# PSUM as one tile of eight banks, MLP units of one bank, and score pieces issued two by two

## The chip, the core and the metric

The kernel runs on one core of a Trainium2 chip. The metric is the device time of one execution in microseconds (us). The core has a matrix engine (TensorE, in the profile PE, and PEld for its weight loads), two engines that read its results out of the accumulation memory PSUM (ScalarE or ACT, VectorE or DVE), a third for work between SBUF tiles (GpSimd or POOL), and SyncE (SP), which here only issues DMAs. PSUM has 128 partitions of eight banks; one bank holds 512 fp32 values for each partition. Engines run their own instruction lists in order and wait for each other through semaphores.

## What is computed

An attention with a few extra keys ("beacons") ahead of the sequence, followed by a two-layer MLP with a squared relu. In short:

```python
# B, H, S, Nb, D = 8, 8, 576, 16, 64;  d_model 512, d_ff 2048
k_all, v_all = concat(beacon_k, k), concat(beacon_v, v)          # 592 keys
a = softmax(q @ k_all.T / sqrt(D), causal on the sequence's keys, beacons always seen)
x = (a @ v_all) as [B*S, H*D]                                    # 4608 tokens x 512
out = (relu(x @ w_in) ** 2) @ w_out                              # 4608 x 512
```

## The kernel before

**Tiling.** Each of the 8 batches is worked in 4 head pairs, so there are 32 pairs. For a pair, PE computes scores transposed (keys on partitions, queries along the row): `qk`, at L506, in matmuls that use 64 of the 128 rows, one head in the upper and one in the lower half. Call this the row form. The scores of a pair come in four *pieces* (batch 0: one and three). A piece holds one or two ranges of queries, so two or four matmuls, and fills a pair of PSUM banks, one bank for each head. ACT takes the exponential of a piece (`exp`, L520), DVE sets masked entries to zero (`mask`, L530 and L534), PE multiplies by v (`av`, L550, 30 matmuls of 65 columns), DVE divides by the sum (`norm`, L565 and L566) into `xn`.

The result of a batch is transposed into the ring `xT`: on PE for batches 0 and 1 (L614), by five DMA transposes on SP for the others (L597). Queries and keys are transposed on PE for batches 0 to 2 (`tp`, L401 and L405, a third form that uses 64 columns), and from batch 3 on they are loaded (L326, L327), cast by POOL (L282) into `qk_area`, and transposed by two DMAs on SP, qT and kT (L359). `qk_area` is first used by PE's transposes; its second use waits for the last of those (a memset on POOL, L306).

The MLP works in 9 chunks of 512 tokens. In the first layer (`s1`, L678) a *unit* is two of the 16 column tiles of w_in, 8 matmuls of 512 columns into a pair of banks; ACT or DVE takes the relu (L694, L696) of 1024 values, and DVE squares it (L703). The second layer (`s2`, L718) adds 16 matmuls for each of 4 groups of 128 tokens; two groups share a pair of banks, ACT copies them out (L280), and SP stores 256 tokens (L750). The last 256 tokens are copied and stored in two halves (L752).

**What sets the order.** A planner (`Order`, L44) plays the program through with a price for each operation and a delay for its result to be seen. At each moment an engine takes the available operation of the lowest number (`prio`); a gate ties the attention's progress to that of the MLP. The order so found is written out, engine by engine, and the chip keeps it. Operations that write PSUM take a buffer from the pool `ps`, four tiles of two banks each, in the order in which they came free; limits say how many each kind may hold:

```python
pools={"ps": range(4), "stg": range(NSTG), "pt": range(NPT)},
limits={"strip": 2, "av": 2, "mlp": 2, "tp": 1},
```

`strip` are the scores, `tp` the transposes. A score piece takes one tile and its exp gives it back (L513 to L524); an MLP unit takes one and its relu gives it back.

Of the kernel before, what the change touches and what calls it, by code (L numbers as in the profile page):

```python
# [9 lines left out]
FP32 = mybir.dt.float32  # L10
# [6 lines left out]
class Op:  # L17
# [4 lines left out]
                 "sync", "insts")  # L22

    def __init__(self, name, engs, dur, emit, prio=0.0, deps=(), take=None, give=None,
                 gate=None, dma=0.0, pe_time=0.0, behind=(), sync=()):
# [12 lines left out]
        self.dma = dma  # L38
        self.pe_time = pe_time
        self.behind = list(behind)  # L40
        self.followers = []


class Order:  # L44
# [3 lines left out]
    LAT = {"PE": 0.2, "ACT": 0.2, "DVE": 0.15, "POOL": 0.25, "SP": 0.1, "-": 0.0}  # L48

    def __init__(self, pools, limits):  # L50
        self.pools = {k: list(v) for k, v in pools.items()}
        self.limits = dict(limits)
        self.inuse = {k: 0 for k in limits}
# [9 lines left out]
    def run(self):  # L63
# [23 lines left out]
        now = 0.0  # L87
        while events:
            now = events[0][0]
            while events and events[0][0] <= now + 1e-9:  # L90
# [6 lines left out]
                elif kind == "give":  # L97
                    pool, cls, idx = op.give.held
                    self.pools[pool].append(idx)
                    if cls in self.inuse:  # L100
                        self.inuse[cls] -= 1
            again = True
            while again:
                again = False
                for e in engines:
# [3 lines left out]
                    fallback = None  # L109
                    for op in avail[e]:  # L110
                        if any(free[x] <= now + 1e-9 for x in op.engs[:op.engs.index(e)]):
                            continue
                        if op.take:
                            pool, cls = op.take
                            if not self.pools[pool]:
                                continue
                            if cls in self.limits and self.inuse[cls] >= self.limits[cls]:
                                continue
# [20 lines left out]
                    if op.take:  # L139
                        pool, cls = op.take  # L140
                        op.held = (pool, cls, self.pools[pool].pop(0))
                        if cls in self.inuse:
                            self.inuse[cls] += 1
                    dur = op.dur[e] if isinstance(op.dur, dict) else op.dur
                    end = now + dur
# [31 lines left out]
def kernel(  # L177
# [64 lines left out]
    ps = [psum.tile([128, 2, 512], FP32, name=f"ps{i}") for i in range(4)]  # L242

    def wait_for(later, first):
# [4 lines left out]
        pools={"ps": range(4), "stg": range(NSTG), "pt": range(NPT)},  # L249
        limits={"strip": 2, "av": 2, "mlp": 2, "tp": 1},  # L250
# [60 lines left out]
    def add_load(b, x, c, prio, behind=[], sync=[]):  # L311
# [10 lines left out]
        def emit_load(e):  # L322
            st = stg[ld.held[2]]
            insts = []
            if lo:
# [6 lines left out]
                 prio=prio, take=("stg", "stg"), dma=1.1 * rows / 128, behind=load_chain[-1:] + behind, sync=sync)  # L332
        load_chain.append(ld)

        def emit_cast(e):
            st = stg[ld.held[2]]
# [40 lines left out]
    def add_strided(b, prio):  # L377
# [17 lines left out]
        for pr in range(HP):  # L395
# [3 lines left out]
            def emit_tp(e, pr=pr, h=h, box=box):  # L399
                pp = ps[box["t"].held[2]].bitcast(BF16)  # L400
                nc.tensor.transpose(pp[:, 1, 0:Nb], bks[b % 2][:, h, :], ident[0:Nb, 0:Nb])  # L401
                for half, at, t in ((1, Nb, ks), (0, 0, qs)):
                    for u in range(NS):
# [5 lines left out]
            tp = add(f"tp{b}.{pr}", "PE", 0.8 if b else 1.3, emit_tp, prio=100.0 * (HP * b + pr) - 190,  # L409
                     deps=[bk, loads[pr, "k"], loads[pr, "q"], ident_op] + busy, take=("ps", "tp"))  # L410
            box["t"] = tp

            def emit_k(e, pr=pr, box=box):
                pp = ps[box["t"].held[2]].bitcast(BF16)
# [4 lines left out]
            def emit_q(e, pr=pr, box=box):  # L419
                pp = ps[box["t"].held[2]].bitcast(BF16)  # L420
# [3 lines left out]
            ek = add(f"ek{b}.{pr}", "DVE", 0.9, emit_k, prio=-200.0, deps=[tp])  # L424
            eq = add(f"eq{b}.{pr}", ("DVE", "ACT"), 0.75, emit_q, prio=-199.0, deps=[tp])
# [50 lines left out]
    def add_pair(b, pr):  # L476
# [12 lines left out]
        take_pt = add(f"pt{p}", "-", 0.0, None, prio=100.0 * p, deps=qk_deps, take=("pt", "pt"), gate=gate)  # L489
# [4 lines left out]
    def add_phase(b, pr, p, n, ph, take_pt, qk_deps, gate):  # L494
        base = 100.0 * p + 1000.0 * n
        exps = []
        for i, (mms, off, width) in enumerate(ph.pieces):
            cols = sum(max(96, t1 - t0) for _, t0, t1, _ in mms)
            box = {}

            def emit_qk(e, mms=mms, box=box):
                st = ps[box["qk"].held[2]]
                for c, t0, t1, at in mms:
                    for hj in range(2):
                        hp = slice(64 * hj, 64 * hj + 64)
                        nc.tensor.matmul(  # L506
                            st[:, hj, at:at + t1 - t0],
                            kT[b % 2][hp, pr, 128 * c:128 * c + 128],
                            qT[b % 2][hp, pr, t0:t1],
                            start=True, stop=True,  # L510
                        )
# [6 lines left out]
            def emit_exp(e, off=off, width=width, box=box):  # L518
                st = ps[box["qk"].held[2]]
                nc.scalar.activation(pt[take_pt.held[2]][:, :, off:off + width], st[:, :, 0:width],  # L520
                                     AF.Exp, bias=0.0, scale=scale)

            exps.append(add(f"exp{p}.{n}.{i}", "ACT", 0.18 + 2 * width / 1200.0, emit_exp, prio=base + i,
                            deps=[qk], give=qk))  # L524

        def emit_mask(e):
            P = pt[take_pt.held[2]]
# [9 lines left out]
        mask = add(f"mask{p}.{n}", "DVE", 0.15 + 0.14 * ph.diag[3] + (0.25 if ph.last else 0.0), emit_mask,  # L537
# [3 lines left out]
        def emit_av(e):  # L541
            P = pt[take_pt.held[2]]
            a = ps[av.held[2]]
            for hj in range(2):
                h = 2 * pr + hj
                for t in tl:
# [10 lines left out]
        av = add(f"av{p}.{n}", "PE", 0.07 + 0.064 * sum(t + 1 for t in tl), emit_av, prio=base - 150,  # L557
                 deps=[mask] + [cast[b, "v", c] for c in range(tl[-1] + 1)] + av_ops[p], take=("ps", "av"),
# [3 lines left out]
        def emit_norm(e):  # L562
            a = ps[av.held[2]][:, :, 0:nt * (D + 1)].rearrange("p h (t d) -> p h t d", d=D + 1)
# [12 lines left out]
        norm_ops[p, n] = add(f"norm{p}.{n}", "DVE", 0.4 + 0.133 * nt, emit_norm, prio=base - 150, deps=deps, give=av)  # L576
# [27 lines left out]
    def add_xt_pe(b):  # L604
        for k, ph in enumerate(phases(b)):
            for pr in range(HP):
# [3 lines left out]
                def emit_tp(e, pr=pr, box=box, ph=ph):  # L610
                    pp = ps[box["t"].held[2]].bitcast(BF16)
                    for t in ph.tiles:
                        n = t_rows(t)
                        nc.tensor.transpose(pp[:, 0, t_start(t):t_start(t) + n],  # L614
# [3 lines left out]
                         deps=[norm_ops[HP * b + pr, k]], take=("ps", "tp"))  # L618
                box["t"] = tp

                def emit_ev(e, pr=pr, box=box, lo=lo, hi=hi):
                    pp = ps[box["t"].held[2]].bitcast(BF16)
                    at = (b * S) % RING
                    copy_on(e, xT[:, pr, at + lo:at + hi], pp[:, 0, lo:hi])

                o = add(f"xte{b}.{k}.{pr}", ("ACT", "DVE"),
                        {"ACT": 0.2 + (hi - lo) / 1200.0, "DVE": 0.12 + (hi - lo) / 960.0}, emit_ev, prio=-110.0,
# [25 lines left out]
    def add_chunk(j):  # L653
# [11 lines left out]
        for f in range(NFT // 2):  # L665
            sqs = []
            for n, (lo_, hi_) in enumerate(parts):
                spans = [(lo_, wrap), (wrap, hi_)] if lo_ < wrap < hi_ else [(lo_, hi_)]
                N = hi_ - lo_
                box = {}  # L670

                def emit_s1(e, f=f, spans=spans, box=box):
                    h = ps[box["s1"].held[2]]
                    for u in range(2):
                        ft = 2 * f + u
                        for lo, hi in spans:
                            for mc in range(NMC):
                                nc.tensor.matmul(h[:, u, lo - spans[0][0]:hi - spans[0][0]],  # L678
# [155 lines left out]
```

## Time and profile before

| | us |
|---|---|
| median of 3 runs (lowest to highest) | 355.35 (355.27 to 355.38) |
| span of the profiled execution | 353.2 |
| PE busy | 334.7 (95%) |
| ACT busy | 193.4 (55%) |
| DVE busy | 148.9 (42%) |
| POOL busy | 85.5 (24%) |

The profiled execution's own time is its span and what lies around it, 2.15 us if it ran like the median. Times in the views count from the span's start. In a timeline a row is start, length, engine, line, operation, tiles, shape and count, and in brackets the idle time before it with what ended it. A matmul's 64*128 are the rows and columns of the array that it uses, and the last shape is what streams through. Ends of matmuls are modelled and overlap the next start, so starts are compared. A few matmul records are missing.

### The profile page before, as it was taken

The page shows a single profiled execution, that of the slowest core. Times are in us where ns is not written, and L with a number is a line of the kernel's source. Part 1 is how long each engine was busy: PE and PEld are TensorE (multiplying, and loading weights), DVE is VectorE, ACT ScalarE, POOL GpSimd, SP SyncE. Part 2 cuts the span into 40 slices and gives each one's busy share as a digit, 9 for nine tenths or more (in the row PEclk, how much of TensorE's full clock was granted, in tenths as well). Part 3 has the DMA queues.
Part 4 walks back from the last instruction along what each step waited for, and adds up shares of the span by engine and source line. Part 5 has one row for each costly group of instructions (what it writes and reads, how often), then busy time and mean ns, then how long its engine had stood idle before and what let it go on. Part 6 is the DMA issues. An engine that isn't in the chain of part 4 may idle for free.

```text
span 353.2 us, 7173 instructions
## 1 busy us (share of the span) xinstructions
PE 334.7 (95%) x2943; PEld 178.6 (51%) x2980; DVE 148.9 (42%) x287; ACT 193.4 (55%) x233; POOL 85.5 (24%) x132
## 2 busy tenths in 40 slices
PE   3789999999999989999999999999999999999994
PEld 2459665554545444444446874445454444444441
DVE  5576674349714455146622753247132302301300
ACT  2686786287555764665745663676634405505602
POOL 7273721209215504133501651000000000000000
PEclk9999999999999999999999999999999999999999
DMA  7999999965969999699989999440013103003003
GB/s 101 183 160 204 223 206 211 201 169 118 206 116 236 223 221 191 138 224 222 251 137 202 248 213 209 115 118 11 0 61 69 59 0 121 0 0 121 0 0 119
DMA packets 137008, 49.49 MB, mean 140 GB/s; under 512 B 123344, under 2 KB 132048, under 8 KB 136976
## 3 DMA queue, kind: packets, MB, share of 16 engines
q1 hardware_dynamic: 127472, 40.09, 53.4%
q0 software_dynamic: 9504, 8.95, 15.7%
q8 instruction: 23, 0.38, 0.5%
q14 instruction: 9, 0.07, 0.1%
HBM read 37.22 MB, written 9.44 MB: 132 GB/s over the span
## 4 chain that ended last, share of the span: by engine, by line
PE 74%; DMA 12%; SPq 5%; ACT 4%; DVE 2%; issue 2%; POOL 1%; ACTq 0%; DVEq 0%; POOLq 0%
PE ps L678 32%; PE ps L718 27%; PE ps L550 7%; PE ps L506 6%; DMA stg<-in_k_dram 4%; DMA stg<-in_v_dram 4%; SPq L597 3%; ACT pt L520 2%; DMA kT<-qk_area 2%; DMA stg<-in_q_dram 1%; SPq L327 1%; DVE kT L282 1%; DMA qk_area<-in_q_dram 1%; PE ps L405 1%; ACT qT L280 1%
## 5 line engine op out<-in xcount | busy, mean ns | idle before, releaser
L678 PE MATMUL ps<-xT,w_in 128*128 128x512 bf16 (+3 forms) x689 | 131.9, 340 | 1.6 <-ACT qT L280 0.6
L718 PE MATMUL ps<-w_out,g 128*128 128x512 bf16 x554 | 129.5, 380 | 1.4 <-issue 0.5
L520 ACT ACTIVATE pt<-ps 128x832 bf16<-128x832 f32 (+4 forms) x128 | 105.3, 865 | 40.7 <-PE ps L506 40.2
L678 PEld LDWEIGHTS <-w_in 128*128 128x128 bf16 x704 | 66.0, 98 | 57.6 <-issue 6.0
L694 ACT ACTIVATE g<-ps 128x1024 bf16<-128x1024 f32 (+2 forms) x65 | 61.8, 951 | 54.0 <-PE ps L678 53.8
L718 PEld LDWEIGHTS <-g 128*128 128x128 bf16 x576 | 53.0, 98 | 65.7 <-issue 5.8
L703 DVE TENSOR_TENSOR g<-g 128x1024 bf16<-128x1024 bf16 (+2 forms) x80 | 53.0, 664 | 77.5 <-ACT g L694 77.0
L530 DVE TENSOR_TENSOR pt<-pt,tri 128x1024 bf16<-128x1024 bf16 (+1 forms) x36 | 24.8, 692 | 50.1 <-ACT pt L520 48.6
L282 POOL CAST qk_area<-stg 128x512 bf16<-128x512 f32 (+2 forms) x50 | 34.6, 704 | 35.0 <-DMA stg<-in_k_dram 18.7
L282 POOL CAST vb<-stg 128x512 bf16<-128x512 f32 (+1 forms) x38 | 26.0, 695 | 69.6 <-DMA stg<-in_v_dram 59.1
L506 PE MATMUL ps<-qT,kT 64*128 64x80 bf16 (+6 forms) x400 | 39.1, 291 | 1.7 <-DMA kT<-qk_area 1.0
L280 ACT COPY osb<-ps 128x1024 f32<-128x1024 f32 (+1 forms) x19 | 18.3, 969 | 40.6 <-PE ps L718 40.3
L550 PEld LDWEIGHTS <-pt 128*128 128x128 bf16 (+1 forms) x960 | 34.5, 99 | 8.8 <-issue 2.5
L550 PE MATMUL ps<-vb,pt 128*128 128x65 bf16 (+1 forms) x960 | 36.5, 196 | 1.9 <-DVE pt L530 0.9
L566 DVE TENSOR_TENSOR xn<-ps,rcp 128x640 bf16<-128x640 f32 (+2 forms) x36 | 27.0, 750 | 1.7 <-DMA xT<-xn 0.4
L506 PEld LDWEIGHTS <-kT 64*128 64x128 bf16 x400 | 13.7, 97 | 24.2 <-issue 18.8
L565 DVE RECIPROCAL rcp<-ps 128x10 f32<-128x10 f32 (+2 forms) x36 | 7.6, 211 | 38.1 <-PE ps L550 36.2
L696 DVE TENSOR_SCALAR g<-ps 128x1024 bf16<-128x1024 f32 (+2 forms) x15 | 15.8, 1053 | 7.8 <-PE ps L678 7.0
L280 ACT COPY qT<-ps 128x576 bf16<-128x576 bf16 x12 | 7.7, 640 | 16.1 <-DVE kT L282 13.0
L282 DVE COPY kT<-ps 128x16 bf16<-128x16 bf16 (+1 forms) x24 | 9.9, 456 | 9.7 <-PE ps L405 7.5
L405 PE MATMUL ps<-ident,qk_area 96*64 96x96 bf16 x288 | 11.1, 233 | 2.9 <-DMA qk_area<-in_k_dram 1.8
L534 DVE TENSOR_TENSOR pt<-pt,tri 80x160 bf16<-80x160 bf16 x32 | 10.8, 339 | 0.0
(31 smaller groups left out, 57.1 us busy)
## 6 DMA issues: line engine op xcount, KB each, us to landing
out_dram<-osb SPq DMA_DIRECT2D x17, 512.0 KB, 3.5
stg<-in_v_dram SPq DMA_DIRECT2D x21, 256.0 KB, 5.1
stg<-in_q_dram SPq DMA_DIRECT2D x20, 256.0 KB, 4.8
stg<-in_k_dram SPq DMA_DIRECT2D x15, 256.0 KB, 5.1
w_in<-in_moe_w_in_dram POOLq DMA_DIRECT2D x4, 512.0 KB, 8.2
w_out<-in_moe_w_out_dram POOLq DMA_DIRECT2D x4, 512.0 KB, 10.6
stg<-in_v_dram SPq DMA_DIRECT2D x7, 224.0 KB, 4.7
qk_area<-in_k_dram POOLq DMA_DIRECT2D x4, 288.0 KB, 12.4
```

The source lines that it names most:

```text
L280: nc.scalar.copy(dst, src)
L282: eng[e].tensor_copy(dst, src)
L506: nc.tensor.matmul(st[:, hj, at:at + t1 - t0], kT[b % 2][hp, pr, 128 * c:128 * c + 128], qT[b % 2][hp, pr, t0:t1], start=True, stop=True,)
L520: nc.scalar.activation(pt[take_pt.held[2]][:, :, off:off + width], st[:, :, 0:width], AF.Exp, bias=0.0, scale=scale)
L530: nc.vector.tensor_tensor(out=d, in0=d, in1=tri[:, m0:m0 + m, :][:, None].to_broadcast([128, 2, m, 128]), op=ALU.min)
L550: nc.tensor.matmul(a[:, hj, (t - tl[0]) * (D + 1):(t - tl[0] + 1) * (D + 1)], P[0:rr, hj, o:o + 128], vb[b % 2][0:rr, c, h, :], start=(c = ...
L566: nc.vector.tensor_tensor(out=xn[b % 2].rearrange("p t (h d) -> p h t d", d=D)[:, 2 * pr:2 * pr + 2, tl[0]:tl[0] + nt], in0=a[:, :, :, 0:D ...
L678: nc.tensor.matmul(h[:, u, lo - spans[0][0]:hi - spans[0][0]], w_in_sb[:, mc, ft * 128:(ft + 1) * 128], xT[:, mc, lo % RING:lo % RING + hi ...
L694: nc.scalar.activation(dst, h, AF.Relu, bias=0.0, scale=1.0)
L696: nc.vector.tensor_scalar(out=dst, in0=h, scalar1=0.0, scalar2=None, op0=ALU.max)
L703: nc.vector.tensor_tensor(out=d, in0=d, in1=d, op=ALU.mult)
L718: nc.tensor.matmul(o[:, ts, :], G[:, fc, (2 * u + ts) * 128:(2 * u + ts + 1) * 128], w_out_sb[:, fc, :], start=(fc == 0), stop=(fc == NFT ...
```

## The change

PSUM becomes one tile of eight banks. A new pool, `Banks`, gives out single banks or aligned pairs: a pair is the lowest free one; a single bank is one whose partner is taken, the lowest of those, or else the lowest free. Limits are counted in banks (scores, attention results and MLP 4 each, transposes 2), and while an operation that wants two pairs lacks banks, operations behind it in rank may bring the MLP to 2 banks only (`floors`).

An MLP unit is now one column tile: 4 matmuls into one bank, with its own relu of 512 values; the square is still taken over two tiles. Each of the 4 token groups of the second layer has its own bank and its own copy out. For chunk 0 the four groups now advance together, quarter by quarter of w_out; before, the first two ended ahead of the last two.

For batches 1 to 7 the scores of a pair are issued as two operations of two pieces each; each takes two pairs of banks, and each of its exps gives back one.

In the planner the delays and prices change, and PE's price gets 0.096 us more wherever the form of its matmuls changes (`mode`).

```diff
+class Banks:
+    def __init__(self):
+        self.free = set(range(8))
+
+    def find(self, wants):
+        left = set(self.free)
+        got = []
+        for n in wants:
+            if n == 2:
+                pick = next((b for b in range(0, 8, 2) if b in left and b + 1 in left), None)
+            else:
+                pick = min(left, key=lambda b: (b ^ 1 in left, b), default=None)
+            if pick is None:
+                return None
+            got.append(pick)
+            left -= {pick, pick + 1} if n == 2 else {pick}
+        return got
...
-    LAT = {"PE": 0.2, "ACT": 0.2, "DVE": 0.15, "POOL": 0.25, "SP": 0.1, "-": 0.0}
+    LAT = {"PE": 0.2, "ACT": 0.15, "DVE": 0.12, "POOL": 0.15, "SP": 0.1, "-": 0.0}
+    DRAIN = 0.096
...
+                            if cls in self.limits:
+                                most = self.limits[cls]
+                                if short is not None and op.prio > short:
+                                    most = min(most, self.floors.get(cls, most))
+                                if self.inuse[cls] + sum(wants) > most:
+                                    continue
...
+                    if e == "PE":
+                        dur += self.DRAIN * (mode not in (None, op.mode))
+                        mode = op.mode
...
-    ps = [psum.tile([128, 2, 512], FP32, name=f"ps{i}") for i in range(4)]
+    ps = psum.tile([128, 8, 512], FP32, name="ps")
...
-        pools={"ps": range(4), "stg": range(NSTG), "pt": range(NPT)},
-        limits={"strip": 2, "av": 2, "mlp": 2, "tp": 1},
+        pools={"ps": Banks(), "stg": Slots(NSTG), "pt": Slots(NPT)},
+        limits={"strip": 4, "av": 4, "mlp": 4, "tp": 2},
+        floors={"mlp": 2},
...
-        for i, (mms, off, width) in enumerate(ph.pieces):
-            cols = sum(max(96, t1 - t0) for _, t0, t1, _ in mms)
+        twos = 2 if b >= NSPLIT else 1
+        for i in range(0, len(ph.pieces), twos):
+            group = ph.pieces[i:i + twos]
+            cols = sum(t1 - t0 for mms, _, _ in group for _, t0, t1, _ in mms)
...
-            qk = add(f"qk{p}.{n}.{i}", "PE", 0.05 + cols / 2400.0, emit_qk, prio=base + i,
-                     deps=qk_deps + [take_pt], take=("ps", "strip"), gate=gate)
+            qk = add(f"qk{p}.{n}.{i}", "PE", cols / 2400.0, emit_qk, prio=base + i,
+                     deps=qk_deps + [take_pt], take=("ps", "strip", [2] * len(group)), gate=gate, mode="rows")
...
-                s1 = add(f"s1.{j}.{f}.{n}", "PE", 1.73 * N / TCH, emit_s1, prio=base + f + 0.5 * n,
...
+                    us = NMC * (0.0024 * len(spans) + N / 2400.0)
+                    s1 = add(f"s1.{j}.{ft}.{n}", "PE", us, emit_s1, prio=base + 0.5 * ft + 0.5 * n,
...
+                             take=("ps", "mlp", [1]), pe_time=us)
...
-                rl = add(f"relu{j}.{f}.{n}", ("ACT", "DVE"), {"ACT": 0.2 + N / 600.0, "DVE": 0.15 + N / 480.0},
-                         emit_relu, prio=-20.0, deps=[s1], give=s1)
+                    rls.append(add(f"relu{j}.{ft}.{n}", ("ACT", "DVE"), {"ACT": act(N), "DVE": dve(N)},
+                                   emit_relu, prio=-20.0, deps=[s1], give=s1))
...
+        step = 4 if j == 0 else 8
+        order2 = ([(ts, f0) for f0 in range(0, NFT, step) for ts in range(4)] if j == 0 else
+                  [(ts, f0) for ts in range(4) for f0 in range(0, NFT, step)])
```

Three places of the order that comes out. The first is PE at the third head pair of batch 3. `w_in` and `xT` are the first layer, `w_out` and `g` the second, `qT` and `kT` scores, `vb` and `pt` the attention's product; each range of queries takes two matmuls, one for each head. Before, the pair's first piece (496 queries) stands alone:

```order
L678 MATMUL ps2_101<-xT_89,w_in_61 128x512
L506 LDWEIGHTS kT1_80
L506 MATMUL ps1_100<-qT1_78,kT1_80 128x496
L506 LDWEIGHTS kT1_80
L506 MATMUL ps1_100<-qT1_78,kT1_80 128x496
L550 LDWEIGHTS pt1_82
L550 MATMUL ps3_102<-vb1_76,pt1_82 128x65
```

And now:

```order
L627 MATMUL ps_99<-vb1_76,pt1_82 128x65
L584 LDWEIGHTS kT1_80
L584 MATMUL ps_99<-qT1_78,kT1_80 128x496
L584 LDWEIGHTS kT1_80
L584 MATMUL ps_99<-qT1_78,kT1_80 128x496
L584 LDWEIGHTS kT1_80
L584 MATMUL ps_99<-qT1_78,kT1_80 128x464
L584 LDWEIGHTS kT1_80
L584 MATMUL ps_99<-qT1_78,kT1_80 128x464
L792 LDWEIGHTS g1_91
L792 MATMUL ps_99<-w_out_62,g1_91 128x512
```

The second piece (464) follows the first directly, behind the attention's product and not ahead of it.

The second place is ACT at the second and third pair of that batch (`pt` are exponentials, `osb` output copies, `g` relus). Before:

```order
L520 ACTIVATE pt1_82<-ps3_102 128x2x496
L520 ACTIVATE pt1_82<-ps1_100 128x2x464
L280 COPY osb0_92<-ps2_101 128x1024
L520 ACTIVATE pt1_82<-ps1_100 128x2x416
L520 ACTIVATE pt1_82<-ps3_102 128x2x288
L694 ACTIVATE g0_90<-ps2_101 128x1024
L520 ACTIVATE pt2_83<-ps1_100 128x2x496
```

And now:

```order
L597 ACTIVATE pt1_82<-ps_99 128x2x496
L597 ACTIVATE pt1_82<-ps_99 128x2x464
L355 COPY osb0_92<-ps_99 128x512 x2
L597 ACTIVATE pt1_82<-ps_99 128x2x416
L597 ACTIVATE pt1_82<-ps_99 128x2x288
L597 ACTIVATE pt2_83<-ps_99 128x2x496
L597 ACTIVATE pt2_83<-ps_99 128x2x464
```

Copies and relus are of 512 values, and two exps always stand together.

The third place is SP's queue from batch 3's last v load on (`stg` are load buffers, the k and q loads are batch 4's). Before:

```order
L327 DMA stg5_68<-in_v_dram 80x8x64
L597 DMA_TRANSPOSE xT_89<-xn0_85 128x4x112
L597 DMA_TRANSPOSE xT_89<-xn0_85 128x4x128 x3
L597 DMA_TRANSPOSE xT_89<-xn0_85 128x4x80
L326 DMA stg6_69<-in_beacon_k_dram 16x8x64
L327 DMA stg6_69<-in_k_dram 112x8x64
L327 DMA stg7_70<-in_q_dram 128x8x64
L327 DMA stg0_63<-in_q_dram 128x8x64
```

And now:

```order
L402 DMA stg5_68<-in_v_dram 80x8x64
L401 DMA stg6_69<-in_beacon_k_dram 16x8x64
L402 DMA stg6_69<-in_k_dram 112x8x64
L402 DMA stg7_70<-in_q_dram 128x8x64
L402 DMA stg0_63<-in_q_dram 128x8x64
L402 DMA stg1_64<-in_q_dram 128x8x64
L402 DMA stg2_65<-in_q_dram 128x8x64
L402 DMA stg3_66<-in_k_dram 128x8x64
L674 DMA_TRANSPOSE xT_89<-xn0_85 128x4x112
L674 DMA_TRANSPOSE xT_89<-xn0_85 128x4x128 x3
L674 DMA_TRANSPOSE xT_89<-xn0_85 128x4x80
```

The transposes of batch 2's result have moved behind seven loads of batch 4.

More of the change, by code (lines that the diff above doesn't have):

```diff
@@ L703, in emit_sq @@
                     nc.vector.tensor_tensor(out=d, in0=d, in1=d, op=ALU.mult)
[L705 removed]
+                sqs.append(add(f"sq{j}.{f}.{n}", "DVE", 0.05 + N / 870.0, emit_sq, prio=-10.0, deps=rls))
             sq.append(sqs)
[L707 to L712 removed]
@@ new lines, in add_chunk, with emit_s2 @@
+        order2 = ([(ts, f0) for f0 in range(0, NFT, step) for ts in range(4)] if j == 0 else
+                  [(ts, f0) for ts in range(4) for f0 in range(0, NFT, step)])
+        for n, (ts, f0) in enumerate(order2):
+            def emit_s2(e, ts=ts, f0=f0):
+                o = bank(s2_first[j, ts])
+                for fc in range(f0, f0 + step):
+                    nc.tensor.matmul(o, G[:, fc, ts * 128:(ts + 1) * 128], w_out_sb[:, fc, :],
+                                     start=(fc == 0), stop=(fc == NFT - 1))
+            o = add(f"s2.{j}.{ts}.{f0}", "PE", MM * step, emit_s2, prio=base + 100 + n,
+                    deps=[x for f in range(f0 // 2, (f0 + step) // 2) for x in sq[f]]
+                    + [w_ops["out", qd] for qd in range(f0 // 4, (f0 + step) // 4)] + [s2_ops.get((j, ts))],
+                    take=None if f0 else ("ps", "mlp", [1]), pe_time=MM * step)
+            if not f0:
+                s2_first[j, ts] = o
+            s2_ops[j, ts] = o
```

241 lines of the change are left out of this document (124 added, 117 removed).

## The prediction

> **What bounds the kernel now.** I read the page first, then the windows, the waits of PE, and PE's timeline.
>
> ```profile
> span 353.2 us, 7173 instructions
> PE 334.7 (95%) x2943; PEld 178.6 (51%) x2980; DVE 148.9 (42%) x287; ACT 193.4 (55%) x233; POOL 85.5 (24%) x132
> ...
> PE 74%; DMA 12%; SPq 5%; ACT 4%; DVE 2%; issue 2%; POOL 1%; ACTq 0%; DVEq 0%; POOLq 0%
> ```
>
> ```profile
> 0.00:28.00 28.00, 18.81 (x278) 12.98 (x279) 16.73 (x58) 17.08 (x25) 16.15 (x31) 1.00 0.93 151
> 28.00:145.00 117.00, 114.06 (x1212) 64.06 (x1225) 63.09 (x117) 73.65 (x95) 42.50 (x62) 1.00 0.99 190
> 145.00:335.00 190.00, 188.35 (x1396) 95.64 (x1417) 68.42 (x112) 99.90 (x111) 26.88 (x39) 1.00 0.53 116
> ```
>
> TensorE is the bound. In the windows the first figure after the length is PE's busy time: 9.2 us of the first 28 are idle, while DMA stands at 0.93, and from 28 to 335 us only 2.94 + 1.65 = 4.6 us. The granted clock is 1.00 in all three. Half of ACT and DVE is free. So there are three places to win: idle time of the start, at most 4.6 us of waits after it, and time inside PE's busy rows.
>
> ```profile
> PE ps L401 <- DVE bks L373: 4.2, 1, 4.2
> ...
> PE ps L506 <- DMA kT<-qk_area: 1.0, 1, 1.0
> ...
> PE ps L678 <- ACT qT L280: 0.6, 1, 0.6
> ```
>
> The first is the start; the other two are the largest single waits after it. The busy rows hold something too:
>
> ```profile
> 270.62 8.80 PE L678 MATMUL ps<-xT,w_in 128*128 128x512 bf16 x39
> 279.26 2.97 PE L718 MATMUL ps<-w_out,g 128*128 128x512 bf16 x13
> ```
>
> ```profile
> 98.35 0.58 PE L506 MATMUL ps<-qT,kT 64*128 64x496 bf16 x4
> 98.86 1.90 PE L718 MATMUL ps<-w_out,g 128*128 128x512 bf16 x8
> 100.70 0.35 PE L506 MATMUL ps<-qT,kT 64*128 64x336 bf16 x4
> 100.98 1.90 PE L718 MATMUL ps<-w_out,g 128*128 128x512 bf16 x8
> 102.81 0.51 PE L506 MATMUL ps<-qT,kT 64*128 64x208 bf16 x6
> ```
>
> Starts are compared, since ends are modelled. 279.26 - 270.62 = 8.64 us for ten units of four matmuls (39 recorded, one missing): 0.216 each. Eight of them take 1.73, yet from 98.86 to 100.70 and from 100.98 to 102.81 it is 1.84 and 1.83: **0.10 is lost where PE goes from the full form (128*128) to the row form (64*128)**. Back it is the same: the piece at 100.70 streams 336 + 80 columns, 416 x 0.216/512 = 0.18 us (its two heads run at once), and the next starts 0.28 later. I take 0.096 for a turn, between 0.09 and 0.11.
>
> **The change, part by part.**
>
> *Score pieces two by two.* Matmuls and weight loads are 2980 each before and after, so no PE work goes or comes; only the turns change. In the orders I count runs of row-form work: 81 before, 66 after. That is fewer than one would think, since in the kernel before many pieces already stood side by side (runs of 8 matmuls are two pieces). Turns between unlike forms, transposes included, fall from 185 to 160. 25 x 0.096 = **-2.4 us** (2.2 to 2.7), all on PE, which is the path.
>
> *MLP units of one bank.* The same 128x512 matmuls in the same count: nothing on PE. Relus go from 80 to 160 and output copies from 19 to 36:
>
> ```profile
> L694 ACT ACTIVATE g<-ps 128x1024 bf16<-128x1024 f32 x54 | 55.3, 1024 | 50.5 <-PE ps L678 50.4
> ...
> L520 ACT ACTIVATE pt<-ps 128x832 bf16<-128x832 f32 x36 | 30.9, 864 | 13.2 <-PE ps L506 13.1
> L520 ACT ACTIVATE pt<-ps 128x928 bf16<-128x928 f32 x32 | 30.3, 948 | 8.8 <-PE ps L506 8.7
> ...
> L280 ACT COPY osb<-ps 128x512 f32<-128x512 f32 x2 | 1.1, 589 | 0.7 <-PE ps L718 0.7
> ```
>
> A half costs 589 against 1024 ns, so 97 splits add 97 x (2 x 0.589 - 1.024) = 15 us of busy time to ACT and DVE, which have 160 and 204 us idle: hidden, as long as no bank comes free too late. Skill and rows can be weighed here. The Trainium skill (Perfetto Trace Analysis, Optimizing Scalar/DVE Operations) says that grouping into larger operations helps a saturated engine, and that breaking them up helps where an engine that is not saturated makes others wait. By its first half the split would cost the 15 us if ACT were full; by its second it costs nothing. At 55% the rows are nearer the second, so the sum takes 0.
>
> *Banks handed out singly, lowest first.* Before, four pairs went round; now the lowest fitting bank is taken, often the one just freed. How tight is that?
>
> ```profile
> 279.46 1.02 ACT L694 ACTIVATE g<-ps 128x1024 bf16<-128x1024 f32 x1 [0.70 <-PE ps L678]
> ```
>
> ```profile
> 25.43 0.87 ACT pt L520
> 26.30 0.04 issue
> 26.34 0.89 PE ps L550 x24
> ```
>
> The relu starts 0.20 us after the last unit's stream ends (279.26), and PE follows 0.04 after an ACT instruction's end (26.30 to 26.34). With the half's 0.59 that makes 0.83 us from a unit's end to its bank's next use, and the next unit streams 4 x 0.216 = 0.86. Two banks in turn just suffice, with 0.03 to spare, if ACT is idle. If it is in an exp it is not. Up to four banks may be with the MLP, which gives 3 x 0.86. So the cost lies between 0 and, at one relu in ten of 160 caught half an exp (0.47) late, 7.5 us; the waits after 28 us that the same banks cost before (at most 4.6) can also shrink by finer release. I take 0, nearest the idle rows.
>
> *The start.* The loads of the first 28 us and POOL's queue keep their order. The first MLP unit stands one attention block and 0.4 us of scores earlier.
>
> ```profile
> 17.36 3.15 POOL L639 DMA_DIRECT2D w_in<-in_moe_w_in_dram  x4 [0.81 <-DMA stg<-in_v_dram]
> ...
> 25.66 0.85 POOL L327 DMA_DIRECT2D stg<-in_v_dram  x1 [1.95 <-DMA w_in<-in_moe_w_in_dram]
> ...
> 26.34 0.89 PE L550 MATMUL ps<-vb,pt 128*128 128x65 bf16 x24 [0.22 <-ACT pt L520]
> ...
> 27.61 0.99 PE L678 MATMUL ps<-xT,w_in 128*128 128x240 bf16 x8
> ```
>
> The first quarter of w_in is there at 25.66, so MLP work can fill the 0.2 to 0.3 us that PE waits for an exp at 26.3: **-0.3 us** (0 to -1).
>
> *Loads on SP.* SP's DMAs are the same, in another order: the five transposes of batch 2's result now go behind seven loads of batch 4, and three of batch 4's v loads behind its q and k transposes.
>
> ```profile
> 72.65 2.71 SPq L750 DMA_DIRECT2D out_dram<-osb  x2
> 81.42 1.36 SPq L327 DMA_DIRECT2D stg<-in_k_dram  x2
> ...
> 91.16 3.10 SPq L359 DMA_TRANSPOSE kT<-qk_area  x1
> ...
> 96.12 6.73 SPq L597 DMA_TRANSPOSE xT<-xn  x5
> ```
>
> ```profile
> DMA to landing us min/median/max: 5.0/6.4/6.9
> ```
>
> ```profile
> 78.31 0.16 PE L401 MATMUL ps<-ident,bks 16*128 16x16 bf16 x1
> ```
>
> ```profile
> 130.51 0.58 PE L506 MATMUL ps<-qT,kT 64*128 64x496 bf16 x4 [0.97 <-DMA kT<-qk_area]
> ```
>
> These are SP's queue, the time to landing of the transposes into kT, and two rows of PE. Batch 3 is the tight place: batch 2's last PE transpose (78.31) frees the area that its casts fill, and kT lands at 91.16 + 5.0 to 6.9, so 17.9 to 19.8 us later; 19.3 at the median. The first scores came 98.35 - 78.31 = 20.0 later. In the new order 0.7 us less PE work lies between, so 19.3: just in time. What is queued ahead counts too: the second store of chunk 0 stands before batch 3's last two k loads as it did, but both its output tiles are now finished together at the chunk's end, so it may hold the loads a microsecond longer, and with them v, qT and kT, all in SP's queue. Batch 4's kT loses 6.7 us of transposes ahead of it in one place and gets them back in the next, and its scores come some 2 us sooner; I leave its 1.0 us. Batches 5 to 7 had microseconds of room. Between -1.0 (batch 4's wait gone) and +4 (both late by 2): **+0.5 us**.
>
> *The end.* Last copies and stores were already split by 512 and stay: 0.
>
> Sum: -2.4 - 0.3 + 0.5 = -2.2 us. The profiled span is 353.20, the median of the runs 355.35; the 2.15 us around the span are left alone. 353.20 - 2.2 = 351.0 in the span, **353.15 us** as a time (-0.6%).
>
> **Rivals.**
>
> *Just-freed banks make PE wait* (slower). For it: a margin of 0.03 us where relu is alone, pieces in twos that put two exps (0.95 and 0.86) in a row before ACT, and 505 waiting PE instructions instead of 450. The Trainium skill (Perfetto Trace Analysis, Matmuls) wants independent matmul groups to rotate through the banks; lowest-first gives that up, and no run here shows it yet. Against it: ACT idle 45%, four banks for the MLP. It decides from 2.2 us on, 14 ns for each of 160 units. At 0.04 us a unit it is 6.4: 355.35 - 2.7 + 6.4 = 359.0.
>
> *kT comes late* (slower). The price above at its end: batch 3 and batch 4 each 2 us late, 355.35 - 2.7 + 4 = 356.7. It decides from 2.7 us of late kT in all.
>
> *Nothing to measure.* Some 2 us of either, together with the turns won: 355.2.
>
> *More is won.* If finer release and the new order also take 3 of the 4.6 us of waits: 355.35 - 2.7 - 3 = 349.7; with half of that, 351.1.
>
> **How the numbers follow.** A measurement of this kernel can tell about 0.2%, 0.7 us, from no change. Forecast (352 to 354.6) 0.45; more won 0.17; nothing to measure 0.13; just-freed banks 0.13; late kT 0.12. So faster 0.62, same 0.13, slower 0.25. The range leaves out the far half of the bank rival and the far end of more won: 350.3 to 357.5.
>
> **What would show it.** Turns: the same 0.10 at each, fewer of them, and 66 row-form runs; a sum of PE starts 2.4 us shorter. Banks: PE waits for ACT at the relu or exp lines with more than about 1 us in total speak for the first rival. Late kT: a PE wait for DMA kT of more than 1.0 us. The start: the first MLP matmul before 27 us. I am wrong if PE's idle time from 28 to 335 us rises above 7 us, or if the turns shrink when pieces stand apart.

## The result and the profile after

The changed kernel takes 349.19 us (median of 4 runs, 348.92 to 349.65) against 355.31 (355.19 to 355.38): ratio 0.9832, 95% interval 0.9818 to 0.9846. That is 6.1 us less where 2.2 less was forecast, and below the range. Beside other kernels on another chip it took 349.07 again.

The page of the changed kernel, and its windows (length, then PE's busy time; ACT's stands fourth):

```profile
span 347.7 us, 7270 instructions
PE 331.8 (95%) x2944; PEld 177.7 (51%) x2980; DVE 150.2 (43%) x306; ACT 202.3 (58%) x311; POOL 84.8 (24%) x132
...
PE 92%; DMA 3%; issue 2%; ACT 1%; DVE 1%; POOL 0%; SPq 0%; ACTq 0%; POOLq 0%
```

```profile
0.00:28.00 28.00, 19.43 (x272) 13.48 (x273) 16.14 (x60) 16.07 (x23) 15.92 (x31) 1.00 0.89 143
28.00:145.00 117.00, 115.06 (x1261) 64.30 (x1274) 63.91 (x130) 78.01 (x125) 45.33 (x66) 1.00 1.08 199
145.00:335.00 190.00, 188.35 (x1379) 96.02 (x1398) 70.17 (x118) 105.87 (x161) 23.59 (x35) 1.00 0.51 111
```

Two things can be read at once. The chain that ended last goes through PE for 92% of its length, before for 74%; DMA fell from 12% to 3% and SP's queue from 5% to 0. And PE's idle time from 28 to 335 us is 3.6 us, before 4.6. Both are too much: 36 matmul records are missing in this trace and 37 in the one before, and a missing record can leave a gap of up to 0.2 us that is none. Two traces lost no record. The first below is experiment 1's, with the order of PE of the kernel before, and shows 2.03 and 0.07 us; the other is experiment 2's, with the order of PE of the changed kernel, and shows 0.19 and 0.02. So some 2.1 us of waits stood there, and 1.9 of them went:

```profile
28.00:145.00 117.00, 114.97 (x1225) 63.98 (x1223) 62.46 (x117) 73.42 (x95) 41.16 (x62) 1.00 1.01 190
145.00:335.00 190.00, 189.93 (x1418) 95.60 (x1417) 68.59 (x112) 100.11 (x111) 26.36 (x39) 1.00 0.57 116
```

```profile
28.00:145.00 117.00, 116.81 (x1265) 64.26 (x1263) 62.95 (x128) 78.70 (x125) 45.50 (x66) 1.00 1.08 200
145.00:335.00 190.00, 189.98 (x1398) 95.97 (x1397) 68.99 (x117) 105.37 (x161) 23.28 (x35) 1.00 0.49 110
```

PE's waits in the changed kernel:

```profile
PE ps L476 <- DVE bks L448: 4.2, 1, 4.2
...
PE ps L480 <- DMA qk_area<-in_q_dram: 1.2, 2, 0.8
PE ps L480 <- DMA qk_area<-in_k_dram: 1.2, 1, 1.2
PE ps L584 <- ACT pt L597: 1.0, 2, 0.8
PE ps L627 <- POOL vb L357: 0.5, 1, 0.5
```

The start's waits are still there. The two largest waits after it, DMA kT (1.0) and ACT qT (0.6), have no row any more. The waits for ACT at L584 are in the start (0.8 of them at 19.8 us).

From start to start, PE's stream (first matmul to last) is 4.5 us shorter: 2.4 are 25 turns between unlike forms, and the other 2.1 are put down to waits. What lies behind the last matmul is another 1.0 shorter, 5.1 before and 4.1 after. The rest of the 6.1, 0.6, is where the two profiled executions stood among their runs.

**The end.** These are ACT and SP of the kernel before from 345 us on:

```profile
346.84 1.01 ACT L280 COPY osb<-ps 128x1024 f32<-128x1024 f32 x1 [11.11 <-PE ps L718]
348.57 1.07 ACT L280 COPY osb<-ps 128x512 f32<-128x512 f32 x2 [0.71 <-PE ps L718]
```

```profile
347.88 0.37 SPq L750 DMA_DIRECT2D out_dram<-osb  x1
349.18 0.85 SPq L752 DMA_DIRECT2D out_dram<-osb  x2
```

And these of the changed kernel:

```profile
342.34 0.58 ACT L355 COPY osb<-ps 128x512 f32<-128x512 f32 x1 [4.58 <-PE ps L792]
344.08 0.59 ACT L355 COPY osb<-ps 128x512 f32<-128x512 f32 x1 [1.15 <-PE ps L792]
```

```profile
342.95 2.09 SPq L817 DMA_DIRECT2D out_dram<-osb  x2
```

Before, both halves of the last unit were copied in a row, x2 in 1.07 us, after its last matmul (348.11). The split by 512 was there, but the first half waited for the whole unit. Now the copy of the third token group starts at 342.34, 1.27 us before the last matmul (343.61), and only one copy and one store stand behind it.

**The turns.** PE in the changed kernel:

```profile
84.20 0.48 PE L584 MATMUL ps<-qT,kT 64*128 64x336 bf16 x8
84.61 1.90 PE L755 MATMUL ps<-xT,w_in 128*128 128x512 bf16 x7
86.44 0.58 PE L584 MATMUL ps<-qT,kT 64*128 64x496 bf16 x4
```

Eight matmuls of 0.216 (one record is missing) from 84.61 to 86.44: 1.83 for 1.73, again 0.10 lost at the turn.

### The profile page after: what moved, and what is told of

Its sections match the earlier page's. It is cut to its first block, busy times and chain, and to the rows that moved or that the text cites. A ratio compares the mean times of both kernels' runs of the same rounds, so it can differ in the third digit from the quotient of the medians.

```text
span 347.7 us, 7270 instructions
## 1 busy us (share of the span) xinstructions
PE 331.8 (95%) x2944; PEld 177.7 (51%) x2980; DVE 150.2 (43%) x306; ACT 202.3 (58%) x311; POOL 84.8 (24%) x132
## 4 chain that ended last, share of the span: by engine, by line
PE 92%; DMA 3%; issue 2%; ACT 1%; DVE 1%; POOL 0%; SPq 0%; ACTq 0%; POOLq 0%
PE ps L755 36%; PE ps L792 36%; PE ps L627 9%; PE ps L584 8%; DMA stg<-in_v_dram 2%; PE ps L480 1%; DMA qk_area<-in_q_dram 1%; PE ps L691 1%; ACT pt L597 1%; DVE pt L607 1%; PE ps L476 0%; DVE g L774 0%; POOL vb L357 0%; ACT osb L355 0%; POOL qk_area L463 0%
## 5 line engine op out<-in xcount | busy, mean ns | idle before, releaser
L792 PE MATMUL ps<-w_out,g 128*128 128x512 bf16 x556 | 127.8, 379 | 2.0 <-issue 1.4
L597 ACT ACTIVATE pt<-ps 128x832 bf16<-128x832 f32 (+4 forms) x128 | 103.8, 869 | 43.9 <-PE ps L584 41.9
L772 ACT ACTIVATE g<-ps 128x512 bf16<-128x512 f32 (+2 forms) x128 | 71.7, 560 | 36.0 <-PE ps L755 34.7
L781 DVE TENSOR_TENSOR g<-g 128x1024 bf16<-128x1024 bf16 (+2 forms) x80 | 51.8, 649 | 71.8 <-ACT g L772 71.0
L355 ACT COPY osb<-ps 128x512 f32<-128x512 f32 x36 | 21.1, 587 | 47.4 <-PE ps L792 41.5
L357 POOL CAST qk_area<-stg 128x512 bf16<-128x512 f32 (+2 forms) x50 | 33.2, 676 | 28.2 <-DMA stg<-in_k_dram 14.8
L584 PE MATMUL ps<-qT,kT 64*128 64x80 bf16 (+6 forms) x400 | 36.4, 291 | 1.0 <-ACT pt L597 1.0
L774 DVE TENSOR_SCALAR g<-ps 128x512 bf16<-128x512 f32 (+2 forms) x32 | 19.6, 612 | 19.3 <-PE ps L755 18.9
L584 PEld LDWEIGHTS <-kT 64*128 64x128 bf16 x400 | 13.0, 97 | 21.1 <-issue 17.5
L480 PEld LDWEIGHTS <-qk_area 96*64 96x64 bf16 x288 | 8.6, 126 | 4.0 <-DMA qk_area<-in_q_dram 2.1
```

Source lines behind the costliest of these rows:

```text
L355: nc.scalar.copy(dst, src)
L357: eng[e].tensor_copy(dst, src)
L480: nc.tensor.transpose(pp[64 * hj:64 * hj + 64, half, at + u * NP:at + (u + 1) * NP], t[b % 2][:, 2 * pr + hj, u, :], ident[0:NP, 0:NP])
L584: nc.tensor.matmul(st[:, hj, at:at + t1 - t0], kT[b % 2][hp, pr, 128 * c:128 * c + 128], qT[b % 2][hp, pr, t0:t1], start=True, stop=True,)
L597: nc.scalar.activation(pt[take_pt.held[0]][:, :, off:off + width], pair(box["qk"], k)[:, :, 0:width], AF.Exp, bias=0.0, scale=scale)
L772: nc.scalar.activation(dst, h, AF.Relu, bias=0.0, scale=1.0)
```

## The experiments

All times are medians. Times and ratios are against the kernel before on the same chip (354.99 to 355.32 there). "Turns" are those between unlike forms in PE's order, 185 in the kernel before and 160 in the changed one. The ratio is not the quotient of the two medians: for the order made with the drain the medians differ by 2.6 us, and the ratio gives 2.9.

| kernel | turns | us | ratio to before, 95% interval |
|---|---|---|---|
| before, first of the last copies on its own | 185 | 354.50 | 0.9981 (0.9971 to 0.9992) |
| before, v loads behind batch 4's kT | 185 | 353.83 | 0.9966 (0.9952 to 0.9979) |
| before, order made with the drain | 175 | 352.39 | 0.9917 (0.9898 to 0.9937) |
| changed, once more | 160 | 349.07 | 0.9824 (0.9809 to 0.9838) |
| changed, end undone | 160 | 349.27 | 0.9838 (0.9822 to 0.9854) |
| changed, longest-free bank | 160 | 348.74, 348.93 | 0.9817 (0.9794 to 0.9840), 0.9823 (0.9808 to 0.9839) |
| changed, drain 0 | 154 | 349.58 | 0.9833 (0.9809 to 0.9857) |
| changed, MLP units of two banks | 159 | 351.01 | 0.9876 (0.9860 to 0.9893) |
| changed, pieces singly | 165 | 351.78 | 0.9909 (0.9882 to 0.9936) |
| changed, both shapes undone | 183 | 353.42 | 0.9940 (0.9923 to 0.9957) |
| changed, pieces singly and drain 0 | 189 | 354.97 | 0.9993 (0.9981 to 1.0006) |

**1. The end, done alone in the kernel before.**

```diff
-                deps = [s2_ops[j, u]]
+                deps = [prevs0 if ts == 0 else s2_ops[j, u]]
...
             prevs[u] = o
+            if u == 1 and n == 5:
+                prevs0 = o
```

> The kernel before with one edit: the first half copy of the last output unit waits for its own token group's last matmul, not for the unit's last one. Theory (the end is a separate 1.0 us of the gain): the two 0.48 us copies no longer stand in a row behind the last matmul and the two last stores no longer overlap, so 0.5 to 1.0 us less, 354.3 to 354.8. Rival (the end gives nothing, as the prediction had it): 355.3.

Measured: 354.50, 0.75 us less (0.3 to 1.0 by the interval). ACT and SP of this kernel from 347 us on:

```profile
348.32 0.59 ACT L280 COPY osb<-ps 128x512 f32<-128x512 f32 x1 [0.71 <-PE ps L718]
```

```profile
347.63 0.37 SPq L752 DMA_DIRECT2D out_dram<-osb  x1
348.93 0.35 SPq L754 DMA_DIRECT2D out_dram<-osb  x1
```

One copy is left behind the last matmul, and what lies behind that matmul is 4.36 us instead of 5.09. The first half's copy has gone ahead, to 341.45. The theory holds: 0.7 us of the gain is the end alone.

**2. The end, undone in the changed kernel.**

```diff
-                               deps=[s2_ops[j, ts]] + st_ops.get(2 * j + u - 2, []), give=s2_first[j, ts]))
+                               deps=[s2_ops[j, 3 if j == NCH - 1 and ts == 2 else ts]] + st_ops.get(2 * j + u - 2, []),
+                               give=s2_first[j, ts], sync=[s2_ops[j, 3]] if j == NCH - 1 and ts == 2 else ()))
```

> The changed kernel with one edit: the first copy of the last two waits again for the last matmul of all. Theory: 0.5 to 1.0 us more, 349.7 to 350.2. Rival (the end gives nothing): 349.2.

Measured: 349.27, by the median only 0.1 to 0.2 more, and the intervals overlap: by the time the theory is not shown here. ACT of this kernel:

```profile
343.05 1.07 ACT L355 COPY osb<-ps 128x512 f32<-128x512 f32 x2 [6.31 <-PE ps L792]
```

The two copies are in a row again, and behind the last matmul lie 4.77 us instead of 4.11, 0.66 more. But in this execution PE's stream before it was 1.0 us shorter (338.4 against 339.4; by the starts of the weight loads it was 0.9 ahead at 28 us), with every engine's instructions in the same order. So the start varies by about the size that was looked for. The end's 0.7 rests on experiment 1 and on both traces.

**3. kT, in the kernel before.** Three load instructions of batch 4's v move behind batch 4's kT in SP's list; no other engine's list changes.

```diff
+        late = [x for x in issued if x[0].name in ("ld4v1", "ld4v2", "ld4v3")]
+        issued = [x for x in issued if x not in late]
+        at = next(i for i, x in enumerate(issued) if x[0].name == "tr4k")
+        issued[at + 1:at + 1] = late
```

> The kernel before, in which only three loads of batch 4's v stand behind batch 4's kT transpose on SP instead of ahead of it; PE, ACT, DVE and POOL keep their rows. Theory (the 1.0 us wait for kT went because the v loads no longer stand ahead of it): kT can go when the last k cast is done, 3 us earlier, the wait of 1.0 to 1.3 us is gone, 354.0 to 354.3. Rival (what the prediction assumed, that kT's wait is set by something else and stays, or v comes late in its place): 355.3 or more.

Measured: 353.83, 1.2 us less (0.7 to 1.7). SP's queue of the kernel before (the store to out_dram stands ahead of the last k loads), then of this one, and PE of this one:

```profile
110.96 0.94 SPq L750 DMA_DIRECT2D out_dram<-osb  x1
112.00 1.90 SPq L327 DMA_DIRECT2D stg<-in_k_dram  x2
...
115.63 3.93 SPq L327 DMA_DIRECT2D stg<-in_v_dram  x4
119.74 4.18 SPq L359 DMA_TRANSPOSE qT<-qk_area  x1
124.03 3.06 SPq L359 DMA_TRANSPOSE kT<-qk_area  x1
```

```profile
117.55 4.31 SPq L363 DMA_TRANSPOSE qT<-qk_area  x1
121.95 2.95 SPq L363 DMA_TRANSPOSE kT<-qk_area  x1
```

```profile
130.72 0.58 PE L510 MATMUL ps<-qT,kT 64*128 64x496 bf16 x4
```

kT is issued 2.1 us earlier, not 3, and the row of PE has no wait. The profiled execution was the longest of twelve (355.14), but the gain stands in it: by the weight loads PE was 1.2 us behind the kernel before ahead of this row, and 0.2 behind it after. The theory holds: the wait was a matter of SP's list. In the changed kernel kT is issued 6 us earlier still:

```profile
110.16 5.61 SPq L434 DMA_TRANSPOSE qT<-qk_area  x1
115.87 3.05 SPq L434 DMA_TRANSPOSE kT<-qk_area  x1
```

```profile
126.11 0.58 PE L584 MATMUL ps<-qT,kT 64*128 64x496 bf16 x4
```

Its scores start 10.2 us after the issue, and before 6.5 after it, with a wait. The scores came 4.4 us earlier, kT's issue 8.2.

**4. The order made with the drain, in the kernel before.** PE's operations get a mode, and the planner adds 0.096 us where it changes; old units, old banks, all other prices old.

```diff
+                    if e == "PE":
+                        dur += 0.096 * (mode not in (None, op.mode))
+                        mode = op.mode
```

> The kernel before with its order made at a drain of 0.096 us, nothing else: 175 turns against 185. Theory (each turn is 0.096 us on the path): 1.0 us less, 354.3. Rival (the other places of the order take it back): 355.3 or more.

Measured: 352.39, 2.6 us less by the medians and 2.9 by the ratio (2.2 to 3.6): more than either theory gave, and over 40% of the whole gain, without a change in any unit. Turns give 1.0 of it. kT is issued at 120.19 instead of 124.03, and PE has no wait for it (1.0). The 0.6 us wait of the MLP for ACT qT at 45 us is gone too. Together that is 2.6, as the medians have it; the two profiled executions are 2.1 apart (353.2 and 351.1), so 0.5 was lost elsewhere in this one. Which place of the order ended the wait for qT no experiment isolates. In experiments 1 and 3, with PE's order of the kernel before, it was 0.33 and 0.76.

**5. MLP units of two banks, in the changed kernel.** Relu and copies of 1024 again, score pieces still two by two.

```diff
-                for ft in (2 * f, 2 * f + 1):
-                    box = {}
...
-                             take=("ps", "mlp", [1]), pe_time=us)
+                         take=("ps", "mlp", [2]), pe_time=us)
...
-                        h = bank(box["s1"])[:, 0:hi - lo]
+                    h = pair(box["s1"])[:, :, 0:hi - lo]
```

> The changed kernel with MLP units of two banks again (relu of 1024, output copies of 1024 but for the last two), score pieces still two by two, the same prices of the order and the same end. PE's stream has 159 turns between unlike forms against 160. Theory (the 2.1 us of PE waits were won by the finer release of banks): they come back wholly or in half, 350.2 to 351.2. Rival (they were won by the new order and its prices): 349.1, the turn less.

Measured: 351.01, 1.9 us more than the changed kernel, though with a turn less. PE's waiting rows in this kernel from 73 to 88 us, and ACT at the second of them:

```profile
74.00 1.89 PE L755 MATMUL ps<-xT,w_in 128*128 128x512 bf16 x8 [0.31 <-ACT osb L355]
...
81.14 1.89 PE L755 MATMUL ps<-xT,w_in 128*128 128x512 bf16 x8 [0.70 <-ACT g L772]
...
87.42 1.89 PE L755 MATMUL ps<-xT,w_in 128*128 128x512 bf16 x8 [0.70 <-ACT g L772]
```

```profile
78.10 1.83 ACT L597 ACTIVATE pt<-ps 128x992 bf16<-128x992 f32 x2 [0.62 <-PE ps L584]
80.06 1.02 ACT L772 ACTIVATE g<-ps 128x1024 bf16<-128x1024 f32 x1
```

The relu of 1024 has to stand behind the two exps (to 79.93) and ends at 81.08; PE goes on at 81.14. The three rows are 0.31 + 0.70 + 0.70 = 1.7 us. Not all of the 1.9 us lies in the span: in all five runs of this kernel 2.0 to 2.1 us lie around it (351.01 for a span of 348.9), against 1.7 in most runs of the others. So the span grew by some 1.5 at the median, and the three rows cover that. Why more lies around it stays open. The waits are not those that the kernel before had (kT and qT), so the theory is only half right: small units did not remove old waits, they keep the pieces two by two from making new ones.

**6. Pieces singly and a drain of 0, in the changed kernel.**

```diff
-    DRAIN = 0.096
+    DRAIN = 0.0
...
-        twos = 2 if b >= NSPLIT else 1
+        twos = 1
```

> The changed kernel with the score pieces singly again and the order made with a drain of 0: 189 turns between unlike forms against 160, banks and end as changed. Theory (each turn is 0.096 us on the path, wherever it stands): 29 more turns are 2.8 us more, 352.0. Rival (turns standing apart cost less, or waits shrink by as much since single pieces hold fewer banks): 349.2 to 350.5.

Measured: 354.97, so 5.9 us more than the changed kernel, where turns alone give 2.8. The turns have their price: median excess from start to start, from 28 us on, 96 ns into the row form and 92 ns out of it, against 96 and 92 in the changed kernel. Of the other 3 us, 2 are one row:

```profile
132.60 0.58 PE L584 MATMUL ps<-qT,kT 64*128 64x496 bf16 x4 [2.02 <-DMA kT<-qk_area]
```

**7. A drain of 0 alone.** The first of the two edits above.

> The changed kernel with its order made at a drain of 0: 154 turns between unlike forms against 160. Theory (turns alone): 6 x 0.096 less, 348.6. Rival (the order's places decide more than its turns, as with single pieces, where waits grew by some 4 us beside 2.8 us of turns): 350 or more, and the profile then shows which wait.

Measured: 349.58, by the medians 0.4 to 0.5 more than the changed kernel and not less, though the intervals overlap (the ratios are 0.9833 here, 0.9832 and 0.9824 there). In the trace the six turns are worth 0.6 us less, yet PE's stream is 0.2 to 0.4 longer (339.6 against 339.4 and 339.2), so 0.8 to 1.0 is lost to waits, 0.35 of it for DMA kT, which had been free. Neither expectation was met, and no difference is shown: the turns saved don't appear in the time.

**8. Pieces singly, drain priced.** The second of the two edits.

> The changed kernel with one edit: score pieces singly, the drain of 0.096 us still priced. 165 turns against 160; on SP four v loads of batch 4 and a store now stand ahead of its kT, as in the kernel with single pieces and a drain of 0. Theory (turns and kT's place): 5 x 0.096 = 0.5 and a kT wait of some 2 us, 351.7. Rival (the pieces two by two are themselves what the change wins, all 2.4 us of turns): 351.6 without a kT wait. Rival (turns alone): 349.7.

Measured: 351.78, as the first theory has it, with the wait that it names, and kT issued late on SP. The profiled execution was the longest of six (354.73), so the wait may be less in others.

```profile
131.62 0.98 PE L584 MATMUL ps<-qT,kT 64*128 64x496 bf16 x4 [2.36 <-DMA kT<-qk_area]
```

```profile
119.96 4.17 SPq L434 DMA_TRANSPOSE qT<-qk_area  x1
124.86 4.65 SPq L434 DMA_TRANSPOSE kT<-qk_area  x1
```

**9. Both shapes undone.** Pieces singly as in 8, MLP units of two banks as in 5.

> The changed kernel with both shapes undone: score pieces singly and MLP units of two banks; new prices, drain and end stay. 183 turns against 160, one v load ahead of batch 4's kT. Theory (turns alone, no kT wait): 23 x 0.096 = 2.2 more, 351.4, so hardly worse than with the pieces two by two and units of two banks (351.0). Rival (units of two banks cost waits of their own, as the 1.9 us at 74 to 87 us did): 353.3.

Measured: 353.42, 4.3 more than the changed kernel, as the rival has it, but not for its reason. No PE wait for ACT between 74 and 88 us is longer than 0.3. PE waits for kT again, 1.5 us at 128.94, and 0.6 for a later batch's at 197.51: the 2.0 that turns alone leave, though this execution was the longest of six (355.17). With one v load ahead of it, kT is issued at 123.96 all the same, since qT ahead of it took 5.7 us. So I read the wait from the wrong sign. Over the traces, issue of batch 4's kT at 123.96 or later goes with a wait of 1.0 to 2.4 us, issue at 122.06 or earlier with 0.4 at most, whatever stands ahead.

**10. The longest-free bank.**

```diff
-                pick = min(left, key=lambda b: (b ^ 1 in left, b), default=None)
+                pick = min(left, key=lambda b: (b ^ 1 in left, self.since[b]), default=None)
```

and the same for pairs; `since` counts up with each bank given back. All engines keep their lists.

> The changed kernel with another choice of banks: of the free ones that which has been free longest, not the lowest. All engines keep their rows, only the addresses differ. Theory (lowest-first costs nothing, since a unit finds up to four banks): 349.2, within 0.4. Rival (just-freed banks make PE wait; rotating takes the 1.0 us of PE's waits for ACT away and some of the small ones): 348.2 or less.

> The changed kernel with the bank that has been free longest, again, now beside the changed kernel on one chip. Theory (lowest-first costs nothing): the same as the changed kernel within 0.3 us. Rival (rotating saves PE's waits for ACT): 0.5 us or more below it.

> The changed kernel itself, for comparison with the rotating one on the same chip. Every theory: 349.2.

Measured: 348.74, and beside the changed kernel on one chip 348.93 against 349.07: the same. PE's waits for ACT in the first run with this edit:

```profile
PE ps L590 <- ACT pt L603: 0.5, 2, 0.3
```

They fell from 1.0 to 0.5, all in the start, and the time doesn't show it. The second run's trace has a wait of 0.6 for a later batch's kT (at 192.18), which the changed kernel's own traces don't have, so such a wait can come and go with one order. Lowest-first costs nothing that can be measured here. The Trainium skill (Perfetto Trace Analysis, Matmuls) wants independent matmul groups to rotate through the banks, so that emptying one overlaps with filling the next; here eight banks handed out singly do that with either pick.

## Why the prediction was wrong, and where it was right

**Score pieces two by two, -2.4: right in size, but not the pieces' alone.** 25 turns at 0.096 are in the trace, and the median price of one is the same in the kernels before and after, 92 to 96 ns. The prediction gave all 25 to the pieces. With a drain of 0 the pieces do take 35 turns off (189 to 154). With the drain priced they take 5 off (165 to 160) where MLP units have one bank, and 24 (183 to 159) where they have two. The price alone takes 10 off in the kernel before (185 to 175). So pieces, units and price can each stand in for the others in part.

**MLP units of one bank, 0: the busy time was there and hidden, but the step priced it as a cost only.** ACT and DVE grew by 8.9 + 1.3 = 10.2 us of the 15, and PE waits for none of it after the start. What the step did not say is that with units of two banks the time is 1.9 us longer when pieces go two by two (experiment 5). The Trainium skill (Perfetto Trace Analysis, Optimizing Scalar/DVE Operations) says that breaking operations up helps where an unsaturated engine makes others wait: ACT is at 58%, and 1.7 us of PE's waits in experiment 5 bear it out.

**Banks handed out singly, 0 of 0 to 7.5: right as to cost.** The rival of just-freed banks (359.0) fell: after the start PE has no wait of 0.2 us or more for ACT in the changed kernel's traces, and the pick makes no difference.

**The start, -0.3: within what can't be told.** The first MLP matmul stands at 25.90, ahead of 27, and PE's idle time of the first 28 us is 8.6 for 9.2. It is 8.9 in the kernel run once more, and two executions of one order stood 0.9 us apart at 28 us (experiment 2).

**Loads on SP, +0.5: wrong, and the sign too.** This is the first step that failed. Three v loads go behind batch 4's transposes, as the prediction said itself; it then counted only the five xT transposes, which go and come back, gave the v loads no price, and left the 1.0 us wait. What came is the lower end of its own range, -1.0. The 4 us at the other end had no ground either. At batch 3, the "tight place", kT made no wait: it was issued at 84.87 instead of 91.16. The stores of chunk 0 did not hold batch 3's last k loads longer (76.23 instead of 81.42), and chunk 0's four groups went quarter by quarter before as well. SP's queue of the changed kernel:

```profile
76.23 1.00 SPq L402 DMA_DIRECT2D stg<-in_k_dram  x2
...
84.87 3.66 SPq L434 DMA_TRANSPOSE kT<-qk_area  x1
```

Batch 4's wait went, worth 1.0 us in the trace and 1.2 in experiment 3. The step failed because it did not work out when batch 4's kT could be issued: 124.03 before, 115.87 after.

**The end, 0: wrong.** "Last copies and stores were already split by 512 and stay" took the split for independence. The profile had shown otherwise in a row that the prediction quotes for another purpose: two copies of 589 ns, x2, with one wait of 0.7 for PE ahead of both. What came was 0.7 to 1.0 us less.

**The other waits, no term: wrong.** The prediction showed the 0.6 us for ACT qT among the largest waits, and its sum gave nothing for it. It went, as it did in the kernel before with the drain's price alone. Only the rival *more is won* allowed for it, and at 349.7 it came nearest. In part that was luck: of the 4.6 us of waits that it drew on, the complete trace of experiment 1 has some 2.1, the rest being mostly gaps of missing records. The 2.1 went nearly whole, and the end made up what was short.

**Around the span, 2.15 left alone.** In later runs of the kernel before, which have both, 1.7 to 1.8 us lie around the span (355.13 for a span of 353.4), and as much in the changed kernel (349.44 for 347.7). With 1.7 the profiled execution of the kernel before would have been 354.9, 0.4 below its median. The forecast takes its 2.2 off either way and does not suffer by it. But the two traces account for 5.5 us, and no row gives a cause for the other 0.6.

Put together: -2.4 turns, -1.0 kT, -0.6 qT and -0.5 of small waits and the start, -1.0 the end, -0.6 the places of the two executions: -6.1. The -0.5 has no experiment of its own, and of the end's 1.0 the last 0.3 was seen only between the two traces. The new delays and the other new prices were never tried alone.

## What to carry to other kernels

Where an order is planned, a missing price (here 0.096 us for a turn) can be worth as much as new units, but what it is worth depends on them. It won 2.6 to 2.9 us in the kernel before and some 3 in the changed kernel with single pieces (354.97 to 351.78), and no more than 0.5 with pieces two by two (349.58 to 349.07). Both shapes undone together cost 4.3 of the 6.1. Such gains don't add up, since each works through the whole order; try a part with and without the others before you credit it. A wait for a transfer is judged by when its instruction can be issued, on its own queue, against when its result is wanted; a list of what stands ahead of it does not tell. And a split of the last copy wins only if each part waits for its own matmuls: look in the trace whether the first part starts before the last matmul ends.

## What the runs showed of the hardware

The turn between the full form and the row form costs PE nearly the same at every place: in eight traces the median is 96 ns into the row form and 92 to 93 ns back, the middle half of the turns lies between 92 and 103 ns, and between like forms nothing is lost over some 2000 pairs in each. Not expected was how far executions of one order differ. PE's stream of the changed order was 338.4, 339.2 and 339.4 us in three traces. By the weight loads, at 28 us the first stood 0.9 us ahead of the longest and the second 0.5 behind it, and PE waits for loads in that stretch. Between 80 and 110 us the longest then lost 0.6 to both. What is smaller than a microsecond was better read from the rows than from the medians.
